# TensorE in program order within attention, and the sums that spread a tile's inverses moved to just ahead of its last value products

## The chip, the cores and the metric

The kernel runs on one core of a Trainium2 chip. A core has five instruction queues that work side by side: TensorE (PE, matrix products; its weight loads are listed apart as PEld), VectorE (DVE), ScalarE (ACT), GpSimdE (POOL) and SyncE (SP, which here issues the DMA transfers). Each of them takes its instructions in the order in which they were written into its queue, and waits for semaphores that others raise. The metric is the device time of one execution in microseconds.

## The reference

Three stages follow one another, on 4 x 576 = 2304 tokens of width 512 (8 heads of 64):

```python
# attention: causal, window of 128, linear bias by distance and head
scores = scale * q @ k.T + slope[h] * -abs(rel);  masked unless 0 <= rel < 128
attn = exp(scores - max);  attn /= sum(attn) + 1e-9
x = attn @ v
# mixture: 8 experts, all of them for every token, weighted by P
P = exp(x @ w_gate - max), then 8 rounds of row and column normalisation
out = sum over e of P[:, e] * (relu(x @ w1[e]) @ w2[e])
# a last two-layer stage
h = out @ w_in;  y = max(0.01 * h, h) @ w_out
```

## The kernel before

**Tiles and steps.** Attention works on 18 tiles of 128 tokens. A tile is done in two steps, `quad` 0 and 1, of four heads each: 36 steps, numbered here 0 to 35. For a step the kernel does, in this order of the data:

- `scores` (L238): four products, two heads `n` by two halves `r` of the partitions, into two PSUM tiles `s[0]` and `s[1]`. The two heads of a PSUM tile use the same 64 rows of TensorE, the two PSUM tiles different ones. Then per head a VectorE operation (L243) that adds the bias and finds the minimum, and a ScalarE exponential (L247) that also sums a row. They write `e`.
- `probs_T` (L273, L275): eight transposes of `e` on TensorE into two PSUM tiles `pt`, and two ScalarE copies from these to `pb`.
- `values` (L288): eight products of `pb` and `v` into `o`. After a tile's second step a VectorE operation (L296) multiplies `o` by the inverse row sums and writes the tile `acc[i]`.
- `inverses`, once for each tile: ScalarE adds a small number to the row sums (L256), VectorE takes the reciprocal (L257), eight small products (L260) spread it over the partitions into `rt`, and ScalarE copies that to `rb` (L263).

**Other work in the same stretch.** A list `fill` holds what the next stage needs: the scaling of the first expert's weights (ScalarE L550, L553, L427; GpSimdE L428, L577), the inputs' parts and sums, and the expert's products for the first token groups (TensorE L702 and L819, 12 or 6 to a piece, and L327 for the gate). The loop over the steps takes it out in portions, before and after the transposes:

```python
        filling(left)
        if scales:
            scales.pop(0)()
        probs_T(i, quad)
        if quad == 1:
            inverses(i)
        filling(left - 1)
        if scales:
            scales.pop(0)()
        values(i, quad)
```

Ahead of these lines stands `scores` of the step after. What the program's order gives one step, from one `scores` to the next, is called a turn below: scores of step k+1, fill, transposes of step k, fill, values of step k.

**What sets the order on an engine.** Not the program's order alone. A scheduler, which has a timeline of its own, places the instructions of each engine's queue, and may put an instruction ahead of earlier ones as long as the data allow it. After attention (L927) the experts' stage goes on for the rest of the span with products of L702 and L819.

**Buffers that tie the steps.** There are two PSUM tiles for `s`, so the scores of a step need the VectorE operations of the step before to be done; two for `pt` and `rt` together; one for `o`.

Of the kernel before, what the change touches and what calls it, by code (L numbers as in the profile page):

```python
# [31 lines left out]
def attn_moe_kernel(  # L32
# [83 lines left out]
    anchors = {}  # L116

# [105 lines left out]
    def scores(i, quad):  # L223
# [28 lines left out]
    def inverses(i):  # L252

        c = st[i]
        sm = c["sm"]
        nc.scalar.activation(out=sm, in_=sm, func=AF.Copy, bias=EPS)  # L256
        nc.vector.reciprocal(out=sm, in_=sm)  # L257
        rt = ps_t.tile([P, NP, P], F32, tag="pt", name="rt")
        for h in range(H):
            nc.tensor.matmul(rt[64 * (h % 2):64 * (h % 2) + 64, h // 2, :], sm[:, h:h + 1].to_broadcast([P, D]), ident,  # L260
                             start=True, stop=True)
        rb = c["rb"] = ap1.tile([P, NP, P], F32, tag="rb", name="rb")
        nc.scalar.activation(out=rb, in_=rt, func=AF.Copy)  # L263

    def probs_T(i, quad):
# [3 lines left out]
        for r in range(2):  # L269
            pt = ps_t.tile([P, 2, 2, P], F32, tag="pt", name="pt")  # L270
            for n in range(2):
                for b in range(nb):
                    nc.tensor.transpose(pt[:, n, b, :], c["e"][r][:, n, b * P:(b + 1) * P], ident)  # L273
# [4 lines left out]
    def values(i, quad):  # L278
# [5 lines left out]
        for n in range(2):  # L284
            for b, j in enumerate(kb):
                for r in range(2):
                    h = 4 * quad + 2 * n + r
                    nc.tensor.matmul(  # L288
# [4 lines left out]
                    )  # L293
# [22 lines left out]
    def logits(p):  # L316
# [6 lines left out]
        for s, terms in enumerate((first, second)):  # L323
            for k in range(n):
                todo = [(o, w, k0, i) for o, w, k0 in terms for i in range(4)]
                for m, (o, w, k0, i) in enumerate(todo):
                    nc.tensor.matmul(lp[:, s, k, :], XP[p][:, o, i // 2, i % 2, k * P:(k + 1) * P], w[:, k0 + i // 2, :],  # L327
                                     start=(m == 0), stop=(m == len(todo) - 1))
# [338 lines left out]
    def a_steps(ci, p):  # L667
# [6 lines left out]
        def step(g, j, d):  # L674
# [22 lines left out]
            for f in range(nf):  # L697
                ft = g * nf + f
                i = 0
                for kk in range(2):  # L700
                    for wp, xp in ((0, 0), (0, 1), (1, 0)):
                        nc.tensor.matmul(d[b][:, f, :], t[:, wp, kk, ft * P:(ft + 1) * P], XP[p][:, o, kk, xp, :],  # L702
                                         start=(i == 0 and f == 0 and j in FIRST), stop=(i == 5), skip_group_check=True)
# [94 lines left out]
    def b_steps(ci, p):  # L798
# [5 lines left out]
        def step(tt, j, d):  # L804
# [11 lines left out]
            for ft in range(2):  # L816
                h, f = Ht[ci, p, ft]
                for hp, wp in ((0, 0), (0, 1), (1, 0)):
                    nc.tensor.matmul(ps, h[:, o, hp, f, tt * P:(tt + 1) * P], w[:, wp, ft, :],  # L819
                                     start=(i == 0 and j in FIRST), stop=(i == 5), skip_group_check=True)  # L820
# [73 lines left out]
    for s, (i, quad) in enumerate(steps):  # L894
# [186 lines left out]
```

## Time and profile before

| what | value |
|---|---|
| median of 3 runs | 1959.84 us (1954.84 to 1960.63) |
| the profiled execution | 1959.59 us, span 1957.8 us |
| TensorE, share of the span | 97% |
| ScalarE, VectorE, GpSimdE | 70%, 67%, 68% |
| granted TensorE clock, mean | 0.995 |
| last value products of attention end | about 232 us into the span |

The span runs from the first to the last instruction; 1.8 us lie around it. Busy shares are averages over stretches with different limits; attention is the first eighth of the span, and the rest is the experts' stage, in which TensorE is busy nearly all the time.

### The profile page before, as it was taken

To read this page: it belongs to the slowest core of one execution; us is meant where nothing else is said; L and a number is where in the kernel's file an instruction comes from. 1 tells how busy PE (TensorE), PEld (TensorE's weight loads), DVE (VectorE), ACT (ScalarE), POOL (GpSimd) and SP (SyncE) were. 2 spreads that over 40 slices of the span, in tenths; PEclk is the share of its full clock that TensorE was granted. 3 is DMA by queue.
4 is the path that set the end of the run, shared out by engine and by line. 5 is a ranking of instruction groups with operands and counts; after the bars stand their busy time and mean duration, and the time that the engine had idled before them with its cause. 6 is when DMAs were issued, how large, how long until landed. Compare 5 with 4: busy or idle time off the path is not lost.

```text
span 1957.8 us, 45103 instructions
## 1 busy us (share of the span) xinstructions
PE 1890.2 (97%) x17725; PEld 1626.5 (83%) x17725; DVE 1320.9 (67%) x3604; ACT 1366.5 (70%) x3123; POOL 1327.3 (68%) x1142
## 2 busy tenths in 40 slices
PE   8999988999999999999999999999999998999998
PEld 6777667888898888889888888889889877889897
DVE  6444466676776767677676767666666777677876
ACT  7977666776767666676767676676666778776764
POOL 3843275868787786878677686775767686666743
PEclk9999999999999999999999999999999999999999
DMA  8432001120211211120111112101000000001001
GB/s 269 125 87 71 12 12 55 39 62 32 82 47 47 66 39 55 39 82 28 66 65 40 55 39 66 44 2 45 23 23 23 23 23 23 24 22 44 2 28 71
DMA packets 57861, 97.80 MB, mean 50 GB/s; under 512 B 3632, under 2 KB 22064, under 8 KB 57648
## 3 DMA queue, kind: packets, MB, share of 16 engines
q1 hardware_dynamic: 57648, 94.92, 14.9%
q8 instruction: 138, 2.26, 0.5%
q14 instruction: 75, 0.61, 0.1%
HBM read 81.81 MB, written 13.11 MB: 48 GB/s over the span
## 4 chain that ended last, share of the span: by engine, by line
PE 78%; ACT 7%; DVE 5%; DMA 5%; POOL 3%; issue 2%; POOLq 0%; SPq 0%; ACTq 0%; DVEq 0%
PE t L819 35%; PE s L702 21%; PE sq L702 15%; DMA raw<-in_moe_w_dram 3%; PE s L238 2%; PE o L288 2%; PE pt L273 1%; ACT junk L550 1%; POOL h L775 1%; DVE s L731 1%; PE rt L260 1%; ACT raw L553 1%; ACT w L427 1%; ACT e L247 1%; ACT xp L427 1%
## 5 line engine op out<-in xcount | busy, mean ns | idle before, releaser
L819 PE MATMUL t<-w,h 128*128 128x256 f16 x7560 | 985.1, 273 | 22.9 <-ACT part L829 10.3
L702 PEld LDWEIGHTS <-w 128*128 128x128 f16 x8400 | 759.1, 98 | 120.3 <-issue 35.0
L819 PEld LDWEIGHTS <-h 128*128 128x128 f16 x7560 | 730.2, 98 | 125.6 <-issue 33.9
L702 PE MATMUL s<-xp,w 128*128 128x256 f16 (+1 forms) x4908 | 620.3, 263 | 20.3 <-ACT q L726 10.4
L832 DVE SCALAR_TENSOR_TENSOR acc<-t,pu,acc 128x256 f32<-128x256 f32 x864 | 407.9, 479 | 220.3 <-PE t L819 173.3
L775 POOL TENSOR_TENSOR h<-s,h 128x1024 f16<-128x1024 f32 x180 | 388.2, 2157 | 136.8 <-ACT h L772 95.7
L702 PE MATMUL sq<-xp,w 128*128 128x256 f16 (+1 forms) x3492 | 447.5, 262 | 6.2 <-ACT q L714 4.5
L830 POOL TENSOR_TENSOR acc<-acc,part 128x256 f32<-128x256 f32 x324 | 235.6, 729 | 292.9 <-ACT part L829 260.6
L428 POOL TENSOR_TENSOR w<-raw,w 128x512 f16<-128x512 f32 x240 | 277.7, 1168 | 42.3 <-ACT w L427 41.9
L731 DVE SCALAR_TENSOR_TENSOR h<-sq,h 128x512 f16<-128x512 f32 (+1 forms) x348 | 190.6, 552 | 82.4 <-ACT h L756 47.6
L829 ACT ACTIVATE part<-t,pu 128x256 f32<-128x256 f32 x324 | 152.5, 471 | 109.0 <-PE t L819 100.1
L772 ACT ACTIVATE h<-s 128x1024 f16<-128x1024 f32 x180 | 189.6, 1053 | 42.2 <-DVE s L731 41.3
L718 DVE SCALAR_TENSOR_TENSOR sq<-sq,q 128x256 f32<-128x256 f32 x348 | 148.4, 427 | 72.0 <-PE sq L702 57.0
L714 ACT ACTIVATE q<-s 128x256 f32<-128x256 f32 x366 | 138.3, 379 | 73.0 <-PE s L702 60.4
L427 ACT ACTIVATE w<-raw 128x512 f16<-128x512 f32 x240 | 148.2, 628 | 8.3 <-PE t L819 6.0
L731 DVE SCALAR_TENSOR_TENSOR s<-sq,s 128x256 f32<-128x256 f32 x348 | 145.1, 417 | 2.1
L750 ACT ACTIVATE h<-sq 128x512 f16<-128x512 f32 x174 | 103.2, 593 | 55.4 <-PE t L819 28.9
L731 DVE SCALAR_TENSOR_TENSOR s<-sq,q 128x256 f32<-128x256 f32 x348 | 130.3, 416 | 12.4 <-ACT q L726 10.6
L550 ACT ACTIVATE junk<-raw 128x512 bf16<-128x512 f32 x160 | 100.2, 626 | 48.2 <-DMA raw<-in_moe_w_dram 47.1
L718 DVE SCALAR_TENSOR_TENSOR sq<-s,q 128x256 f32<-128x256 f32 x174 | 74.5, 428 | 86.6 <-ACT q L714 78.2
L756 ACT ACTIVATE h<-sq 128x256 f16<-128x256 f32 x174 | 65.9, 379 | 65.1 <-DVE sq L718 58.2
L553 ACT ACTIVATE raw<-raw,sr 128x512 f32<-128x512 f32 x160 | 102.4, 714 | 3.8 <-DVE sr L422 3.4
(137 smaller groups left out, 1785.8 us busy)
## 6 DMA issues: line engine op xcount, KB each, us to landing
raw<-in_moe_w_dram SPq DMA_DIRECT2D x32, 1024.0 KB, 5.1
k_t<-in_k_dram SPq DMA_DIRECT2D x16, 512.0 KB, 3.8
raw<-in_moe_w_in_dram SPq DMA_DIRECT2D x16, 512.0 KB, 3.6
raw<-in_moe_w_out_dram SPq DMA_DIRECT2D x16, 512.0 KB, 3.5
q_t<-in_q_dram SPq DMA_DIRECT2D x18, 256.0 KB, 3.7
v_t<-in_v_dram SPq DMA_DIRECT2D x18, 256.0 KB, 2.7
acc<-in_v_dram SPq DMA_DIRECT2D x18, 256.0 KB, 6.6
out_dram<-acc SPq DMA_DIRECT2D x18, 256.0 KB, 2.0
```

The source lines that it names most:

```text
L427: nc.scalar.activation(out=hi, in_=src, func=AF.Copy)
L428: nc.gpsimd.tensor_tensor(out=lo, in0=src, in1=hi, op=ALU.subtract)
L702: nc.tensor.matmul(d[b][:, f, :], t[:, wp, kk, ft * P:(ft + 1) * P], XP[p][:, o, kk, xp, :], start=(i == 0 and f == 0 and j in FIRST), sto ...
L714: nc.scalar.activation(out=q[:, k], in_=ps, func=AF.Copy, scale=CS)
L718: nc.vector.scalar_tensor_tensor(out=block(k), in0=ps, scalar=CS, in1=q[:, k], op0=ALU.mult, op1=ALU.add)
L731: nc.vector.scalar_tensor_tensor(out=out, in0=in0, scalar=sc, in1=in1, op0=op0, op1=op)
L772: nc.scalar.activation(out=h[:, 3:7, 0, :], in_=d["s"], func=AF.Copy)
L775: nc.gpsimd.tensor_tensor(out=h[:, 3:7, 1, :], in0=d["s"], in1=h[:, 3:7, 0, :], op=ALU.subtract)
L819: nc.tensor.matmul(ps, h[:, o, hp, f, tt * P:(tt + 1) * P], w[:, wp, ft, :], start=(i == 0 and j in FIRST), stop=(i == 5), skip_group_chec ...
L829: nc.scalar.activation(out=part, in_=ps, func=AF.Copy, scale=s)
L830: nc.gpsimd.tensor_tensor(out=dst, in0=dst, in1=part, op=ALU.add)
L832: nc.vector.scalar_tensor_tensor(out=dst, in0=ps, scalar=s, in1=dst, op0=ALU.mult, op1=ALU.add)
```

## The change

Every product of attention, and of the fill within it, is chained to the one written before it, by a dependency that costs no semaphore (both stand on TensorE's queue): on TensorE these instructions keep the program's order. Two small groups are not chained and may stand anywhere: the tiny products of the scaling factors (L402 and L421). The chain ends with attention. Besides, `inverses` is cut in two: its ScalarE and VectorE part now stands ahead of the transposes, its eight products and the copy of them (`spread_inverses`) behind the second portion of fill, right ahead of the value products.

```diff
+    in_order = [None]
+
+    def kept(ins):
+
+        if in_order:
+            if in_order[0] is not None:
+                tc.add_manual_dep(ins.ins, in_order[0],
+                                  mybir.DependencyInfo(mybir.DependencyClass.NoSync, mybir.DependencyReason.DATA),
+                                  reason="in order")
+            in_order[0] = ins.ins.name
...
-                nc.tensor.matmul(s[r][:, n, 0:W], qs[64 * r:64 * r + 64, h // 2, :],
-                                 c["k"][64 * r:64 * r + 64, h // 2, 0:W], start=True, stop=True)
+                kept(nc.tensor.matmul(s[r][:, n, 0:W], qs[64 * r:64 * r + 64, h // 2, :],
+                                 c["k"][64 * r:64 * r + 64, h // 2, 0:W], start=True, stop=True))
...
         nc.vector.reciprocal(out=sm, in_=sm)
+
+    def spread_inverses(i):
+
+        c = st[i]
+        sm = c["sm"]
         rt = ps_t.tile([P, NP, P], F32, tag="pt", name="rt")
...
-        probs_T(i, quad)
         if quad == 1:
             inverses(i)
+        probs_T(i, quad)
         filling(left - 1)
+        if quad == 1:
+            spread_inverses(i)
         if scales:
             scales.pop(0)()
         values(i, quad)
     assert not fill
+    in_order.clear()
```

The products of L260, L273, L288, L327, L702 and L819 are wrapped in `kept` in the same way. The number of instructions is the same on every engine. Because the scheduler works on all queues together, the orders on VectorE, ScalarE, GpSimdE and SyncE change too, all within attention; from about the end of attention on, every queue is the same as before.

TensorE around step 7 (the scores `s_657` and `s_658` are step 7's; `pt_682` and `pt_689` belong to step 6, `s_720` and `s_721` to step 8). Before:

```order
L238 MATMUL s_657<-k_t_421,qs_423 128x256 x2
L273 MATMUL pt_682<-ident_81,e_586 128x128 x2
L238 MATMUL s_658<-k_t_421,qs_423 128x256 x2
L273 MATMUL pt_682<-ident_81,e_586 128x128 x2
L421 LDWEIGHTS onesb_94
L421 MATMUL st_405<-b_388,onesb_94 128x2
L273 MATMUL pt_689<-ident_81,e_587 128x128 x4
L238 MATMUL s_720<-k_t_578,qs_580 128x256 x2
L238 MATMUL s_721<-k_t_578,qs_580 128x256 x2
L402 LDWEIGHTS e_535
L402 MATMUL mt_559<-identb_86,e_535 1x128
L288 MATMUL o_703<-pb_687,v_t_356 64x128
```

And with the change:

```order
L249 MATMUL s_657<-k_t_421,qs_423 128x256
L249 MATMUL s_658<-k_t_421,qs_423 128x256
L249 MATMUL s_657<-k_t_421,qs_423 128x256
L249 MATMUL s_658<-k_t_421,qs_423 128x256
L289 MATMUL pt_682<-ident_81,e_586 128x128 x4
L289 MATMUL pt_689<-ident_81,e_587 128x128 x4
L304 MATMUL o_703<-pb_687,v_t_356 64x128
L304 MATMUL o_703<-pb_694,v_t_356 64x128
```

The four scores stand together, in turn from one PSUM tile and the other, where before they were two pairs with other work between; and the scores of step 8, which stood ahead of step 6's value products, now stand behind all eight of them.

ScalarE around step 6 (`e_586`, `e_587`: exponentials of step 6; `w0`, `w1`: casts of the weights; `raw`: their scaling; `pb`: the copies that the value products need). Before:

```order
L247 ACTIVATE e_586,sm_583<-e_586,mn_582 128x256 x2
L247 ACTIVATE e_587,sm_583<-e_587,mn_582 128x256 x2
L263 ACTIVATE rb_638<-rt_629 128x512
L427 ACTIVATE xp0_118<-acc2_102 128x2x128
L247 ACTIVATE e_659,sm_583<-e_659,mn_656 128x256 x2
L275 ACTIVATE pb_687<-pt_682 128x512
L247 ACTIVATE e_660,sm_583<-e_660,mn_656 128x256
L275 ACTIVATE pb_694<-pt_689 128x512
L247 ACTIVATE e_660,sm_583<-e_660,mn_656 128x256
L553 ACTIVATE raw_234<-raw_234,sr_230 128x512 x4
L247 ACTIVATE e_722,sm_719<-e_722,mn_718 128x256 x2
```

And with the change:

```order
L443 ACTIVATE w0_526<-raw_234 128x512
L258 ACTIVATE e_587,sm_583<-e_587,mn_582 128x256 x2
L291 ACTIVATE pb_620<-pt_615 128x512
L291 ACTIVATE pb_627<-pt_622 128x512
L279 ACTIVATE rb_643<-rt_634 128x512
L443 ACTIVATE w1_737<-t2_699 128x512
L443 ACTIVATE w1_740<-raw_236 128x512
L443 ACTIVATE xp0_118<-acc2_102 128x2x128
L443 ACTIVATE w1_743<-raw_236 128x512
L443 ACTIVATE w1_746<-raw_236 128x512
L443 ACTIVATE w1_749<-raw_236 128x512
L258 ACTIVATE e_659,sm_583<-e_659,mn_656 128x256 x2
```

All fourteen casts of the first weight chunk now stand ahead of step 7's exponentials (`e_659`); before, the first cast stood behind step 8's. `t2_699` and `raw_236` are written by GpSimdE.

VectorE around step 4 (`e` from `s` is one head's bias and minimum, `mn` its read-out; `vmx` reads the values of one tile, `acc_107` those of tile 7, `acc_117` of tile 17). Before, step 4's last three heads are the three `e` rows here (its first stands just ahead of them):

```order
L243 ISA e,mn<-s,dist 128x256
L243 ISA mn 128x1
L221 TENSOR_REDUCE vmx<-acc_107 128x1
L243 ISA e,mn<-s,dist 128x256
L243 ISA mn 128x1
L404 TENSOR_REDUCE k<-mt 1x1
L243 ISA e,mn<-s,dist 128x256
L243 ISA mn 128x1
L221 TENSOR_REDUCE vmx<-acc_108 128x1
```

With the change, this stands ahead of step 4's first head (the last row):

```order
L232 TENSOR_REDUCE vmx<-acc_112 128x1
L232 TENSOR_REDUCE vmx<-acc_113 128x1
L410 TENSOR_REDUCE m<-vmx 128x1
L327 TENSOR_SCALAR wg<-wg,srg 128x32
L232 TENSOR_REDUCE vmx<-acc_114 128x1
L268 RECIPROCAL sm<-sm 128x8
L232 TENSOR_REDUCE vmx<-acc_115 128x1
L328 CAST wgs<-wg 128x4x8
L232 TENSOR_REDUCE vmx<-acc_116 128x1
L232 TENSOR_REDUCE vmx<-acc_117 128x1
L329 TENSOR_TENSOR wgs<-wg,wgs 128x4x8
L254 ISA e,mn<-s,dist 128x256
```

All eighteen reads of the values stand ahead of step 4; before, the last of them stood ahead of step 6.

## Rows read from the trace of the kernel before

**Rows 1.** Busy us (and count) of PE, PEld, DVE, ACT, POOL by stretch; PEclk, DMA.

```profile
20.00:80.00 60.00, 57.75 (x469) 41.52 (x470) 34.54 (x162) 56.84 (x171) 39.79 (x38) 1.00 0.57 178
80.00:190.00 110.00, 109.52 (x1002) 80.44 (x1000) 58.63 (x207) 81.53 (x241) 50.97 (x46) 1.00 0.30 87
190.00:232.00 42.00, 42.00 (x428) 31.30 (x427) 18.05 (x66) 26.82 (x76) 3.17 (x2) 1.00 0.09 26
...
300.00:1950.00 1650.00, 1610.06 (x15213) 1418.26 (x15212) 1161.49 (x3013) 1145.08 (x2497) 1179.79 (x992) 1.00 0.13 42
```

**Rows 2.** The same for line 238 (scores) on TensorE alone: PE busy, clock, DMA.

```profile
80.00:190.00 110.00, 27.86 (x132) 1.00 0.30 87
190.00:232.00 42.00, 6.97 (x34) 1.00 0.09 26
```

**Rows 3.** Timeline of TensorE: start, us, engine, line, operation, out<-in, shapes, count.

```profile
35.67 1.13 PE L238 MATMUL s<-k_t,qs 64*128 64x256 f32 x8
36.73 0.43 PE L288 MATMUL o<-pb,v_t 128*64 128x128 f32 x2
...
37.24 1.09 PE L260 MATMUL rt<-ident,sm 128*64 128x128 f32 x16
38.16 1.04 PE L288 MATMUL o<-pb,v_t 128*64 128x128 f32 x14
39.14 1.13 PE L238 MATMUL s<-k_t,qs 64*128 64x256 f32 x4
...
42.10 0.66 PE L273 MATMUL pt<-ident,e 128*128 128x128 f32 x4
...
144.17 1.47 PE L702 MATMUL s<-xp,w 128*128 128x256 f16 x12
```

**Rows 4.** Timeline behind the first of these scores: VectorE and ScalarE.

```profile
36.84 0.42 DVE L243 CUSTOM_DVE_ANT_0 e<-s,dist 128x256 f32<-128x256 f32 x1
...
37.30 0.51 ACT L247 ACTIVATE e<-e,mn 128x256 f32<-128x256 f32 x1
...
37.81 0.49 ACT L247 ACTIVATE e<-e,mn 128x256 f32<-128x256 f32 x1
```

**Rows 5.** Timeline at 66 us: ScalarE's copy and the value product that waits for it.

```profile
66.09 0.60 ACT L275 ACTIVATE pb<-pt 128x512 f32<-128x512 f32 x1
66.56 0.65 ACT L427 ACTIVATE w<-raw 128x512 f16<-128x512 f32 x1
...
66.74 0.98 PE L288 MATMUL o<-pb,v_t 128*64 128x128 f32 x13 [1.20 <-ACT pb L275]
```

**Rows 6.** Timeline of ScalarE: step 2's exponentials, the first weights; later a scaling of four.

```profile
14.76 0.51 ACT L247 ACTIVATE e<-e,mn 128x256 f32<-128x256 f32 x1 [0.57 <-DVE mn L243]
...
16.22 0.63 ACT L550 ACTIVATE junk<-raw 128x512 bf16<-128x512 f32 x1 [0.37 <-DMA raw<-in_moe_w_dram]
...
54.60 2.56 ACT L553 ACTIVATE raw<-raw,sr 128x512 f32<-128x512 f32 x4
```

**Rows 7.** Timeline of VectorE: one of the heads of step 4; the last of the 18 reads.

```profile
26.32 0.41 DVE L243 CUSTOM_DVE_ANT_0 e<-s,dist 128x256 f32<-128x256 f32 x1
...
35.13 0.66 DVE L221 TENSOR_REDUCE vmx<-acc 128x1 f32<-128x512 f32 x1
```

**Rows 8.** Groups on GpSimdE from 20 to 90 us: count, busy us, mean ns, idle before.

```profile
L428 POOL TENSOR_TENSOR w<-raw,w 128x512 f16<-128x512 f32 x12 | 13.8, 1171 | 0.0
...
L577 POOL TENSOR_TENSOR raw<-raw 128x512 f32<-128x512 f32 x4 | 5.1, 1285 | 0.0
```

**Rows 9.** Timeline of TensorE: the last value products of attention.

```profile
230.88 1.09 PE L288 MATMUL o<-pb,v_t 128*64 128x128 f32 x14
```

**Rows 10.** Timeline of TensorE at 10 us.

```profile
10.46 2.07 PE L238 MATMUL s<-k_t,qs 64*128 64x256 f32 x4
```

**Rows 11.** TensorE right behind attention, by stretch: busy us, granted clock, DMA.

```profile
236.00:238.00 2.00, 1.07 (x13) 0.65 0.00 0
238.00:240.00 2.00, 2.00 (x24) 0.50 0.03 8
```

More of the change, by code (lines that the diff above doesn't have):

```diff
@@ L257, in inverses @@
         nc.vector.reciprocal(out=sm, in_=sm)
+    def spread_inverses(i):
+        c = st[i]
+        sm = c["sm"]
         rt = ps_t.tile([P, NP, P], F32, tag="pt", name="rt")
         for h in range(H):
-            nc.tensor.matmul(rt[64 * (h % 2):64 * (h % 2) + 64, h // 2, :], sm[:, h:h + 1].to_broadcast([P, D]), ident,
-                             start=True, stop=True)
+            kept(nc.tensor.matmul(rt[64 * (h % 2):64 * (h % 2) + 64, h // 2, :], sm[:, h:h + 1].to_broadcast([P, D]), ident,
+                             start=True, stop=True))
         rb = c["rb"] = ap1.tile([P, NP, P], F32, tag="rb", name="rb")
@@ L272, in probs_T @@
                 for b in range(nb):
[L273 removed]
+                    kept(nc.tensor.transpose(pt[:, n, b, :], c["e"][r][:, n, b * P:(b + 1) * P], ident))
             pb = ap3.tile([P, 2, 2, P], F32, tag="pb", name="pb")
@@ L287, in values @@
                     h = 4 * quad + 2 * n + r
-                    nc.tensor.matmul(
+                    kept(nc.tensor.matmul(
                         o[64 * r:64 * r + 64, h // 2, :],
@@ L292, in values @@
                         start=(b == 0), stop=(b == len(kb) - 1),
-                    )
+                    ))
         if quad == 1:
@@ L326, in logits @@
                 for m, (o, w, k0, i) in enumerate(todo):
-                    nc.tensor.matmul(lp[:, s, k, :], XP[p][:, o, i // 2, i % 2, k * P:(k + 1) * P], w[:, k0 + i // 2, :],
-                                     start=(m == 0), stop=(m == len(todo) - 1))
+                    kept(nc.tensor.matmul(lp[:, s, k, :], XP[p][:, o, i // 2, i % 2, k * P:(k + 1) * P], w[:, k0 + i // 2, :],
+                                     start=(m == 0), stop=(m == len(todo) - 1)))
         back = small.tile([P, 1], F32, tag="lb", bufs=1, name="lb")
@@ L701, in step @@
                     for wp, xp in ((0, 0), (0, 1), (1, 0)):
-                        nc.tensor.matmul(d[b][:, f, :], t[:, wp, kk, ft * P:(ft + 1) * P], XP[p][:, o, kk, xp, :],
-                                         start=(i == 0 and f == 0 and j in FIRST), stop=(i == 5), skip_group_check=True)
+                        kept(nc.tensor.matmul(d[b][:, f, :], t[:, wp, kk, ft * P:(ft + 1) * P], XP[p][:, o, kk, xp, :],
+                                         start=(i == 0 and f == 0 and j in FIRST), stop=(i == 5), skip_group_check=True))
                         i += 1
@@ L818, in step @@
                 for hp, wp in ((0, 0), (0, 1), (1, 0)):
-                    nc.tensor.matmul(ps, h[:, o, hp, f, tt * P:(tt + 1) * P], w[:, wp, ft, :],
-                                     start=(i == 0 and j in FIRST), stop=(i == 5), skip_group_check=True)
+                    kept(nc.tensor.matmul(ps, h[:, o, hp, f, tt * P:(tt + 1) * P], w[:, wp, ft, :],
+                                     start=(i == 0 and j in FIRST), stop=(i == 5), skip_group_check=True))
                     i += 1
```

## The prediction

> **What bounds the kernel now.** I read the busy time by stretch first, then TensorE's timeline, then what the other engines do between two TensorE groups of one step. The reader is to see that the change can act in attention alone, the first 232 us of 1957.8: TensorE is 98% busy from 300 us on (1610 of 1650 us, [rows 1]) on queues that the change leaves alone, so what attention gains or loses moves the rest as a block. The last value products end at 230.88 + 1.09 = 232.0 us [rows 9]; that is the number which the change moves. Within attention TensorE shows no idle time from 80 to 232 us, and ScalarE is nearly full (56.84 of 60 us) from 20 to 80 us [rows 1]. Taken alone this says that TensorE is the bound.
>
> The timeline says what fills it. Four scores that run side by side take 1.06 us (a group of eight records, each product being two, from 35.67 to the next start at 36.73); two from one PSUM tile, on the same rows of the array, take as long for half the work (four records, 1.13 us at 39.14) [rows 3]. Line 238 takes 27.86 + 6.97 = 34.8 us for 166 records after 80 us [rows 2], where 166/8 groups of 1.06 would be 22.0. Value products with a first one torn off cost 0.43 us more for it [rows 3]. So TensorE is busy partly because its order is poor, and that order let it run ahead while other engines answered.
>
> **What the change removes.** Pairs become fours: 34.8 - 22.0 = 12.8 us of TensorE after 80 us; about as much before it, where ScalarE is the limit. Torn value products: one start of some 0.35 us in about 25 of 36 steps, 9 us. Some 22 us of TensorE's time in the stretch where it shows no idle time. The inverse sums cost the same 1.09 us [rows 3] in the new place; there they run while the copies are awaited, so I price their move at nothing; without that cover they would cost 18 x 1.05 = 19 us, which they cost before too.
>
> **What it adds: a closed turn.** With program order, the value products of step k wait for the ScalarE copies of step k, and the scores of step k+2 stand behind all of them. ScalarE has the exponentials of step k+1 ahead of these copies (order rows in the section on the change). A turn is then a chain through three engines:
>
> - start of the scores to VectorE's first head 36.84 - 35.67 = 1.17, to the first exponential 37.30 - 36.84 = 0.46 [rows 3, 4];
> - four exponentials at 0.49 each (37.30 to 37.81 is one, with its read-out, [rows 4]): 1.96;
> - first copy 0.47 to the next start, second copy 0.60 to its end, 0.05 to the product (66.09 + 0.60 = 66.69, then 66.74) [rows 5]: 1.12;
> - eight value products, 1.05 (sixteen records: 1.09 for as many at 37.24, [rows 3]), then the next scores.
>
> 1.17 + 0.46 + 1.96 + 1.12 + 1.05 = 5.8 us. TensorE's own work in a turn is 1.06 + 1.1 (eight transposes, twice 0.6 at 42.10) + 1.05, with 1.05 for the inverses in every second turn, and 1.3 for each twelve products of fill (1.47 for twelve less the tail of the last) [rows 3]. That is 3.2 to 4.3 us without fill and 5.8 to 6.9 with 24. A turn costs the larger of the two, and 0.3 to 1.0 more where ScalarE's queue has fill between the exponentials and the second copy. From the changed order, for turns 9 to 34 (the 26 from the scores of step 9 to those of step 35): fourteen turns with 24 products or the like at 6.6; seven with twelve at 6.05; turns 9 and 17 at 5.9 and 5.3; two empty ones at 5.3; turn 34 at 5.9. Sum 92.4 + 42.4 + 11.2 + 10.6 + 5.9 = 162.5 us. From the scores of step 35 to the last value product is one chain of 5.8, then transposes, copies and products again: 9.2.
>
> **The first nine turns.** Here the other queues decide, by the order in which they now stand.
>
> - ScalarE has two `junk` sums, which need the weights that land at 16.2 us, ahead of step 2's exponentials [rows 6]: these start at 17.5 instead of 14.8.
> - VectorE has all reads of the values ahead of step 4. The last was at 35.13 between other work, and step 4's third head at 26.32 [rows 7]. Eight reads of about 0.6 us behind step 3's heads and ahead of step 4's put step 4's first head at some 33.5 us and its exponentials at 34.
> - ScalarE's own queue from there, at 0.49 an exponential, 0.47 a copy, 0.61 a scaling (2.56 for four, [rows 6]) and 0.52 a cast (under the 0.65 of [rows 5]): 7.5 us to step 5, 9.5 to step 6, that is 51.
> - Then the cast `w1_737` waits for GpSimdE. GpSimdE can begin its casts at 40.5, and has ahead of `t2_699` nine casts of 1.17, six sums of 1.29 [rows 8] and two others, 20 us: 60. Two more sums to 62.5, then three casts on ScalarE: step 7's exponentials stand behind all of it and start at 64.5. ScalarE idles some 6 us, and nothing covers it, since step 7 is queued behind.
> - Turn 7 at 5.8, turn 8 at 6.9: scores of step 9 at about 76.
>
> **The sum.** 76 + 162.5 + 9.2 = 247.7 against 232.0: 15.7 us later. One term more: in the first 20 us the same pair of scores takes 2.07 us [rows 10], which at the second level takes 1.13 [rows 3]: TensorE's lower clock. Behind attention it fell to 0.50 after stretches with TensorE busy 1.07 of 2 us [rows 11]. In turns 1 to 9 TensorE has 3 to 4 us of work in 6 to 9; I take half clock in the three of them that the chain decides, 1.06 + 0.5 or so each: 4.5 us. Below it is 0, above it is all nine turns, 14. Total about +20 us: 1957.8 + 20, with the 1.8 around the span 1980 us. The profiled run (1959.59) and the median (1959.84) agree to 0.25 us, so the forecast is the same against the median. The turn is known to some 0.4 us, which over 26 turns is 10, and the early walk to 8: the forecast alone holds 1964 to 2000. The DMA loads of q, k and v change places on SyncE's queue by a few positions; after 20 us the DMA is busy at 0.57 and less [rows 1], so I price that at nothing; a load that came late for one turn would cost its 2 to 3 us once.
>
> The Trainium skill, page "TensorE: Matmul & The Clock Gate", section "Why this matters for your kernels", says that idle gaps between bursts of products put the clock back to half, and advises against them. It speaks against this change; the rows at 10 us and behind attention agree. By it, with half clock in all turns, 14 us in the first nine and 26 x 1.5 in the others would come on top of the 15.7, and the sum would be about 2028.
>
> **Rivals.**
>
> *TensorE was the bound (faster).* For it: no idle time in 152 us, and 22 us of its work go away there. Then the end moves with TensorE's time, and what ScalarE holds early stays as it is: 1959.6 - 22 = 1938. It decides where the copies are done before TensorE comes to the value products, that is where the turn's chain is under the 5.8 to 6.9 of TensorE's work; a chain shorter by 0.6 in all filled turns would do for most of it. Against it: the wait at 66.74, 1.20 us for a copy [rows 5], in a stretch with free choice of order, and nine early turns with no fill at all.
>
> The Trainium skill, page "TensorEngine Tiling (Array Packing)", section "Key Properties", says that tiles on different rows of the array load and multiply in parallel; the 1.06 us for four against two agree. By it alone the sum would be this rival's.
>
> *Early loss and later gain cancel (no change).* Before, the 26 steps from 9 to 35 ran under a TensorE without slack; if turns come out at 5.9 on average, since ScalarE's fill falls into the gaps, 26 x 0.35 = 9 us come back and the clock term is nil: 1959 to 1966.
>
> *The clock stays low through most of attention (slower still).* Each chain then holds scores, values and transposes at double: 1.5 us more in 20 to 26 turns, on top of 15.7 and up to 14 in the early ones: 2010 to 2030. Against it: from turn 10 on TensorE has 75% to 100% of a turn to do.
>
> That the order doesn't do as it says is excluded by the order rows, but for the two small groups that aren't chained.
>
> **How the numbers follow.** Forecast 0.60; TensorE the bound 0.20; cancelled 0.12; low clock 0.08. A measurement of this kernel can tell about 0.3%, 6 us, from no change. Faster by more than that 0.21, within it 0.13, slower 0.66. The range 1948 to 2002 holds the forecast, the cancelled case and the nearer half of the two outer ones, and leaves out about 0.2.
>
> **What would show it.** Four scores together in 1.06 to 1.13 us, TensorE's busy time in attention down by 20 us or more while its end moves from 232 to about 250 us. TensorE's longest waits: value products for the ScalarE copies, in most turns; early, ScalarE waiting for GpSimdE at about 55 to 60 us. Step 4's exponentials from about 34 us, step 9's scores at about 76. Turns of 6 to 7 us in the middle. The prediction is wrong if the value products find their copies done, or if step 9 comes at 60 us or earlier. From 300 us on nothing but a shift.

## The result, and the profile after

Over four runs of each on the same chip the changed kernel takes 1983.37 us (1982.27 to 1984.06) against 1958.91 (1954.84 to 1960.63): a ratio of 1.0127, 95% interval 1.011 to 1.0145, so 1.3% slower. The forecast was 1980, in a range of 1948 to 2002.

The page of the changed kernel, its span, the busy time of the engines, and two of its lines in 40 slices of the span (a slice is 50 us; digits are tenths):

```profile
span 1982.3 us, 45132 instructions
...
PE 1870.0 (94%) x17725; PEld 1622.6 (82%) x17725; DVE 1314.3 (66%) x3604; ACT 1365.7 (69%) x3123; POOL 1327.2 (67%) x1142
...
PE   6788888999999999999999999999999999999998
...
PEclk8799989999999999999999999999999999999999
```

TensorE does the same 17725 products in 20.2 us less busy time (1890.2 before), and the span is 24.5 us longer (1957.8 before). The low digits stand in the first slices alone. The busy time by stretch, in the columns of [rows 1] and in answer to them:

```profile
20.00:80.00 60.00, 41.22 (x283) 30.60 (x279) 24.28 (x109) 40.59 (x114) 38.89 (x37) 0.74 0.47 154
80.00:190.00 110.00, 96.20 (x1030) 76.97 (x1030) 50.85 (x199) 79.16 (x235) 41.75 (x38) 1.00 0.25 73
190.00:232.00 42.00, 34.70 (x346) 26.75 (x343) 19.02 (x83) 28.79 (x90) 11.75 (x11) 1.00 0.30 89
...
300.00:1975.00 1675.00, 1630.02 (x15415) 1435.46 (x15413) 1174.30 (x3051) 1157.31 (x2523) 1199.57 (x1010) 1.00 0.13 41
```

From 20 to 80 us TensorE did 283 products instead of 469, and no engine is full: ScalarE, 56.84 of 60 us before, has 40.59. From 300 us on TensorE is 97% busy (98% before). The scores alone, in answer to [rows 2]: more of them fall into these two stretches now, and they take less.

```profile
80.00:190.00 110.00, 16.91 (x126) 10.68 (x128) 1.00 0.25 73
190.00:232.00 42.00, 8.34 (x60) 4.82 (x56) 1.00 0.30 89
```

25.25 us for 186 records are 1.09 us for eight: the fours. The timeline of TensorE in turns 7 to 10 (a turn is named by the step whose scores stand at its head), in answer to [rows 3]:

```profile
57.24 1.82 PE L249 MATMUL s<-k_t,qs 64*128 64x256 f32 x8
58.99 1.09 PE L289 MATMUL pt<-ident,e 128*128 128x128 f32 x8
64.86 2.45 PE L304 MATMUL o<-pb,v_t 128*64 128x128 f32 x16 [4.78 <-ACT pb L291]
67.24 1.94 PE L249 MATMUL s<-k_t,qs 64*128 64x256 f32 x8
...
89.01 1.09 PE L276 MATMUL rt<-ident,sm 128*64 128x128 f32 x16
89.94 1.04 PE L304 MATMUL o<-pb,v_t 128*64 128x128 f32 x16
90.91 1.14 PE L249 MATMUL s<-k_t,qs 64*128 64x256 f32 x8
```

At 60 us TensorE stands still for 4.78 us, ahead of value products that want a ScalarE copy, and the next scores come behind them; at 67 us they take 1.94 instead of 1.1, at the lower of the two clocks (1.2 instead of 2.4 GHz; granted 0.50 from 64 to 68 us). The reason that the copy is late is this piece of ScalarE's timeline: a weight cast `w` waits for GpSimdE, step 7's exponentials (L258) stand behind all five weight casts, and step 6's copies `pb`, which the value products want, stand behind these exponentials.

```profile
59.27 0.63 ACT L443 ACTIVATE w<-t 128x512 f16<-128x512 f32 x1 [3.03 <-POOL t L593]
59.81 0.62 ACT L443 ACTIVATE w<-raw 128x512 f16<-128x512 f32 x1
60.33 0.40 ACT L443 ACTIVATE xp<-acc 128x256 f16<-128x256 f32 x1
60.64 1.73 ACT L443 ACTIVATE w<-raw 128x512 f16<-128x512 f32 x3
62.27 0.49 ACT L258 ACTIVATE e<-e,mn 128x256 f32<-128x256 f32 x1
...
64.23 1.06 ACT L291 ACTIVATE pb<-pt 128x512 f32<-128x512 f32 x2
```

Who waits for whom in attention, 0 to 260 us (us in total, times, longest):

```profile
...
ACT e L258 <- DVE mn L254: 40.3, 24, 4.9
DVE e L254 <- PE s L249: 31.0, 26, 4.7
...
PE o L304 <- ACT pb L291: 18.4, 19, 4.8
PE rt L276 <- ACT pb L291: 15.5, 11, 4.8
```

These are three sides of one ring: TensorE waits 33.9 us for ScalarE's copies, VectorE 31.0 for scores, ScalarE 40.3 for VectorE's minima.

Where the time goes is seen best from the start of the first value product of a step. The table has it for all kernels of this study (each from its profiled execution; the medians and ratios are against runs of the kernel before on the same chip, 1956.8 to 1958.9 us).

| kernel | step 8 | step 11 | from step 11 to 35 | last values end | median | ratio to before (95%) |
|---|---|---|---|---|---|---|
| before | 58.7 | 75.9 | 154.3 | 232.0 | 1958.9 | 1 |
| changed | 82.5 | 103.7 | 154.2 | 259.0 | 1983.4 | 1.0127 (1.0110 to 1.0145) |
| fours alone | 65.9 | 84.8 | 147.7 | 233.5 | 1954.9 | 0.9993 (0.9980 to 1.0005) |
| chain, inverses in the old place | 82.6 | 106.5 | 163.8 | 271.4 | 1994.2 | 1.0184 (1.0169 to 1.0200) |
| changed, scores two steps ahead | 64.0 | 104.4 | 144.4 | 249.8 | 1972.8 | 1.0078 (1.0063 to 1.0093) |
| changed, reads held back | 75.5 | 104.7 | 153.5 | 259.2 | 1980.7 | 1.0119 (1.0103 to 1.0134) |
| changed, second weights tied | 76.2 | 108.3 | 155.1 | 264.4 | 1985.8 | 1.0147 (1.0131 to 1.0163) |
| scores ahead, weights tied | 61.5 | 99.3 | 141.9 | 242.2 | 1964.2 | 1.0040 (1.0025 to 1.0055) |
| before, weights tied | 58.8 | 79.9 | 149.1 | 230.8 | 1944.7 | 0.9942 (0.9924 to 0.9959) |
| chained from step 10 | 58.0 | 93.1 | 154.1 | 248.3 | 1972.1 | 1.0080 (1.0061 to 1.0100) |
| chained up to step 9 | 81.2 | 104.9 | 145.8 | 253.7 | 1974.7 | 1.0091 (1.0068 to 1.0114) |
| changed, products added | 88.7 | 109.4 | 155.0 | 265.5 | 1986.6 | 1.0150 (1.0132 to 1.0168) |
| chained from 10, fill free | 59.2 | 78.5 | 153.7 | 233.3 | 1954.7 | 0.9985 (0.9976 to 0.9995) |
| before, tied, late fours | 58.7 | 77.6 | 146.6 | 225.2 | 1945.2 | 0.9944 (0.9927 to 0.9960) |

The loss is 23.8 us at step 8 and 27.8 at step 11. In between it grows to 34.4 at step 23, and at step 35 it is 27.7 again: over the middle as a whole, though not turn by turn, a chained turn is as long as a step was before. The end of attention moves by 27.0, the whole kernel by 24.5, so some 2 us come back behind attention; in the other chained kernels of the table the whole time moves by 2 to 5 us less than the end of attention.

### The profile page after: what moved, and what is told of

Its sections match the earlier page's. It is cut to its first block, busy times and chain, and to the rows that moved or that the text cites. A ratio compares the mean times of both kernels' runs of the same rounds, so it can differ in the third digit from the quotient of the medians.

```text
span 1982.3 us, 45132 instructions
## 1 busy us (share of the span) xinstructions
PE 1870.0 (94%) x17725; PEld 1622.6 (82%) x17725; DVE 1314.3 (66%) x3604; ACT 1365.7 (69%) x3123; POOL 1327.2 (67%) x1142
## 4 chain that ended last, share of the span: by engine, by line
PE 71%; ACT 9%; DMA 6%; POOL 5%; DVE 5%; issue 3%; SPq 0%; POOLq 0%; DVEq 0%; ACTq 0%
PE t L835 34%; PE s L718 19%; PE sq L718 14%; DMA raw<-in_moe_w_dram 4%; ACT e L258 2%; ACT junk L566 2%; POOL w L444 1%; PE o L304 1%; POOL h L791 1%; DVE s L747 1%; PE s L249 1%; ACT raw L569 1%; DMA acc<-in_v_dram 1%; PE rt L276 1%; POOL xp L444 1%
## 5 line engine op out<-in xcount | busy, mean ns | idle before, releaser
L747 DVE SCALAR_TENSOR_TENSOR s<-sq,q 128x256 f32<-128x256 f32 x348 | 129.9, 414 | 12.1 <-ACT q L742 10.6
L734 DVE SCALAR_TENSOR_TENSOR sq<-s,q 128x256 f32<-128x256 f32 x174 | 74.4, 428 | 85.7 <-ACT q L730 77.3
```

The costliest lines, as they stand in the source:

```text
L734: nc.vector.scalar_tensor_tensor(out=block(k), in0=ps, scalar=CS, in1=q[:, k], op0=ALU.mult, op1=ALU.add)
L747: nc.vector.scalar_tensor_tensor(out=out, in0=in0, scalar=sc, in1=in1, op0=op0, op1=op)
```

## The experiments

The theories: (1) the **closed turn** of the prediction, value products that wait for their own step's copies with the next scores behind them; (2) **early queues**, the orders on VectorE, ScalarE and GpSimdE in the first nine turns; (3) the move of the inverses; (4) the lower clock. One more came up on the way: (5) the **fill in the chain**, expert products whose inputs come late from GpSimdE and which all of attention now stands behind.

Moving the inverses without the chain leaves every engine's order of instructions as it was before, so that kernel wasn't run: the move can act only together with the chain.

**Fours alone.** Before, with the four scores of a call chained to each other and to nothing else:

```diff
     def scores(i, quad):
+        in_order[0] = None
         for n in range(2):
-            for r in range(2):
-                nc.tensor.matmul(s[r][:, n, 0:W], ...
+            for r in (1, 0):
+                kept(nc.tensor.matmul(s[r][:, n, 0:W], ...
```

> The kernel before, with one thing of the change: the four scores of one call are chained to each other and nothing else is, so the products of other kinds may stand between the calls as before. It tells what fours are worth without the closed turn. Rival 'TensorE was the bound': scores' busy time after 80 us falls from 34.8 us to between 22 and 30 (not all calls come out as fours, since the scheduler decides what stands between), and the whole time falls by that, 5 to 12 us against the kernel before. Closed turn (the loss of the change comes from value products that wait with the scores behind them): no loss here, time within 6 us of the kernel before or below it, attention ends at 220 to 234 us. If this run is 20 us slower, the order of the scores alone does the harm and both are wrong.

No difference that can be told. The steps from 11 to 35 are 6.6 us shorter, but 8.9 us were lost up to step 11. The scores took 32.77 us for 175 records after 80 us, against 34.8 for 166: few calls came out as full fours. TensorE's products become cheaper and the time stays. Why the first steps lose time isn't shown.

**The inverses in their old place.** The changed kernel, with

```diff
-        if quad == 1:
-            inverses(i)
         probs_T(i, quad)
-        filling(left - 1)
         if quad == 1:
+            inverses(i)
             spread_inverses(i)
+        filling(left - 1)
```

> The changed kernel with the inverses back in their old place (both halves between the transposes and the second portion of fill), all products still chained. It tells the chain from the move of the inverses. Closed turn and early queues alike: the chain does it, and the time stays within 8 us of the changed kernel's 1983. The moved inverses as the cause: back to about 1960. The prediction's price for the move was nothing, which asks for a difference under 6 us.

11 us slower still: outside what either theory expected, and outside the prediction's price of nothing for the move. The waits on TensorE in all of attention in this kernel:

```profile
PE rt L276 <- ACT pb L291: 23.6, 16, 6.4
PE o L304 <- ACT pb L291: 20.5, 18, 4.0
```

44.1 us for the two together against 33.9 in the changed kernel. The inverses take a PSUM tile of the same two as the transposes, so they wait for a copy of these; in the chain the fill that could run meanwhile stands behind them. The move is worth 10 us under a chain, and cannot be the cause of the loss.

**Scores two steps ahead.** The changed kernel, with

```diff
     scores(*steps[0])
+    scores(*steps[1])
...
-            scores(*steps[s + 1])
...
+        if s + 2 < len(steps):
+            scores(*steps[s + 2])
         values(i, quad)
```

> The changed kernel, but the scores are written two steps ahead: those of steps 0 and 1 before the loop, those of step s+2 right ahead of the value products of step s, so that they no longer stand behind products that wait for ScalarE's copies. Chain and moved inverses stay. Closed turn: it is opened, the 172.8 us from the scores of step 9 to those of step 35 shrink towards TensorE's own work (about 146 to 155 us), attention ends at 222 to 238 us and the time is 1945 to 1962. Early queues alone (the loss is made by the orders on VectorE, ScalarE and GpSimdE in the first nine turns, where those engines are waited for): the scores of step 9 still come after 70 us and the time is 1972 to 1985.

10.5 us back. The time lies just within what early queues alone had, but their sign fails: step 9's scores came at 56.4, not after 70. Values of step 8 come at 64.0 instead of 82.5, which is 18.5 of the 23.8 us lost up to there, and from step 11 on it is 9.8 us faster than the changed kernel. The 18.5 us aren't the closed turn's alone, though: the edit moves the other queues as well, and ScalarE has two weight casts ahead of step 7's exponentials here, where the changed kernel has fourteen. No run opens the turn and leaves these orders as they were. And all that was won early is gone at step 11. TensorE's timeline in this kernel, then GpSimdE's, then ScalarE's:

```profile
65.51 0.83 PE L718 MATMUL s<-xp,w 128*128 128x256 f16 x6
81.64 0.37 PE L718 MATMUL s<-xp,w 128*128 128x256 f16 x1 [15.30 <-ACT xp L443]
83.84 1.23 PE L718 MATMUL s<-xp,w 128*128 128x256 f16 x5 [1.83 <-POOL xp L444]
```

```profile
74.67 2.25 POOL L444 TENSOR_TENSOR w<-raw,w 128x512 f16<-128x512 f32 x2
76.89 0.71 POOL L490 TENSOR_TENSOR sx<-acc,sx 128x256 f32<-128x256 f32 x1
77.57 2.25 POOL L444 TENSOR_TENSOR w<-raw,w 128x512 f16<-128x512 f32 x2
79.79 0.71 POOL L490 TENSOR_TENSOR sx<-acc,sx 128x256 f32<-128x256 f32 x1
81.67 2.12 POOL L444 TENSOR_TENSOR xp<-sx,xp 128x1024 f16<-128x1024 f32 x1 [1.17 <-ACT xp L443]
```

```profile
80.54 1.06 ACT L443 ACTIVATE xp<-sx 128x1024 f16<-128x1024 f32 x1 [6.28 <-POOL sx L490]
```

The first expert products want `xp`, the split inputs of the first token groups; their sums `sx` stand on GpSimdE between weight casts `w`, and the last is done at 80.5. All attention that is ready to run waits behind these products. This is where theory 5 comes from.

**Reads held back.** The changed kernel, with VectorE's eighteen `vmx` reads tied behind the heads of the scores written last:

```diff
-        nc.vector.tensor_reduce(out=vmx[:, i:i + 1], in_=acc[i], ...
+        ins = nc.vector.tensor_reduce(out=vmx[:, i:i + 1], in_=acc[i], ...
+        if heads:
+            tc.add_manual_dep(ins.ins, heads[-1].ins.name, ...
```

> The changed kernel, with the eighteen VectorE reads of the values tied behind the heads of the scores written last, so that they can't all stand ahead of step 4's heads. Nothing else is altered. Early queues: step 4's exponentials start at about 28 to 31 us instead of 33.6, and the time falls by 2 to 6 us, to 1977 to 1981. Closed turn alone, or if ScalarE and GpSimdE bind the first nine turns in any case: step 9's scores stay at 77 us and the time within 2 us of 1983.

Step 4's exponentials start at 32.6 instead of 33.6, later than the 28 to 31 expected. Step 9's scores come at 70.2 instead of 77.3 (here nine casts, not fourteen, stand ahead of step 7's exponentials), with the turn still closed; then the chain waits for the inputs again (ScalarE 5.26 us for GpSimdE's `sx` at 76 to 81 us), the values of step 11 come 1.0 us later than in the changed kernel, and attention ends within 0.2 of it. The whole time is 2.7 us lower, within what two such comparisons can differ by. So the early queues set part of the pace of the first nine turns, but mending them in this way only brings the wait for the inputs forward.

**Second weights tied behind the inputs.** The changed kernel, with the casts and sums of the first expert's second weight matrix (`W[1][0].whole()`, eleven jobs on GpSimdE) written behind the first token groups' inputs and held there on ScalarE and GpSimdE:

```diff
-    fill = ... + W[1][0].scale() + W[1][0].whole()
+    fill = ... + W[1][0].scale()
...
                     fill += xin[p].parts(1) + a_steps(0, p) + [lambda p=p: logits(p)]
+                if p == 0:
+                    fill += W[1][0].whole() + [W[1][1].load]
...
+        if late:
+            behind(c, 0)
+            behind(s, 1)
```

> The changed kernel, with the seven casts and four sums of the first expert's second weight matrix tied behind the split inputs of the first token groups on ScalarE and GpSimdE (they stood ahead of part of them). TensorE's chain is left as it is, but for the later place of no product at all. Theory 'inputs behind weights': the first expert products in the chain wait for inputs whose sums and casts stand on GpSimdE behind weight casts that nothing needs yet, and all of attention waits behind these products. In this kernel the waits of the closed early turns still hide most of that, so by it step 9's scores come at 70 to 75 us instead of 77.3, attention ends at 252 to 257 us instead of 259.0 and the time is 1975 to 1981. Closed turn alone: the first turns are as long as they were, time within 2 us of 1983.

A miss for theory 5 as I had put it. Step 9's scores did come at 71.9, but the casts now run beside the first expert block, where they hold up VectorE (below, on the hardware); the chained products wait 3.98 us for ScalarE at 92.7 to 96.7, and step 12's scores come at 102.5 instead of 97.8. **The same with the scores ahead:**

> Both edits: scores written two steps ahead, and the second weight matrix's casts and sums tied behind the first split inputs. With the scores ahead alone, step 10's scores came at 62.0 us and step 11's at 89.6, and between them TensorE waited 15.3 us for a ScalarE cast of the inputs. Theory 'inputs behind weights': that stall shrinks from some 20 us above a usual turn to 8 or less, step 11's scores come at 68 to 78 us, attention ends at 227 to 238 us, and the time is 1950 to 1962, so no slower than the kernel before. Rival: the inputs can't come sooner, since attention's own values, or TensorE's chain before them, set their time; then step 11's scores stay at 86 to 90 us and the time at 1970 to 1975.

8.7 us better than the scores ahead alone, a little short of what was expected: the wait for ScalarE's cast of the inputs shrank from 15.30 to 5.26 us, and step 11's scores came at 79.2 instead of 89.6. **And the control, the kernel before with the same tie:**

> A control: the kernel before, with the same tie of the second weight matrix's casts behind the first inputs and no chain on TensorE. There the scheduler has the inputs ahead of nearly all weight casts already, and TensorE can take other products while it waits. By 'inputs behind weights' the edit is worth nothing here, 1952 to 1962. A gain of over 6 us would say that the tie is a gain by itself and that its worth in the other two kernels says nothing on the chain.

It gains 12 us by itself, which I had not expected. By what I had written, the worth of the tie in the other two says nothing on the chain then. What does is the shrunk wait in the trace, and the place of the gain: with the scores ahead the tie ends attention 7.6 us earlier (242.2 for 249.8). Here the gain isn't in attention's end (1.2 us earlier); some 6 us of it are there by 640 us, as the 4000th expert product comes at 641.9 instead of 648.0, and the rest between 640 and 1080 us (8000th: 1070.5, was 1084.1). TensorE's mean granted clock over the span is 0.998, against 0.995, but that isn't the main part: one run of the kernel before had 0.998 too and took 1955.7 us. Why a tie in attention speeds up the later stage stays open.

**Chain in one part alone.** The changed kernel with the chain begun at step 10 (`in_order` empty until then), and with the chain ended there:

```diff
+        if s == 10:
+            in_order.append(None)       # the other kernel: in_order.clear()
```

> The changed kernel, chained from step 10 on only; the steps 0 to 9 are as free as before, and TensorE's order up to about the scores of step 10 is that of the kernel before. Moved inverses stay. Theory 'early steps': the loss of the change is made before step 11, where ScalarE, VectorE and GpSimdE are behind and the chain turns each of their late results into a stall of all that follows; from step 11 on a chained turn lasts as long as a step did before (154.2 against 154.3 us from the values of step 11 to those of step 35). Then this kernel ends attention at 228 to 237 us and takes 1952 to 1963. Closed turn as the cause throughout (values that wait in every turn, with the next scores behind them): the 25 chained turns lose most of the 27 us by themselves, and the time is 1970 to 1982.

> The other half: the changed kernel, chained up to step 9 and free from step 10 on. Theory 'early steps': the loss is there already, values of step 8 at 78 to 86 us as in the changed kernel (82.5), attention ends at 250 to 260 us and the time is 1974 to 1985. Closed turn throughout: most of the loss is gone, 1957 to 1968. Both together would put it in between.

Chained up to step 9: the loss at step 8 is there, as "early steps" had it, and the free part behind makes up 8.5 us. Chained from step 10: steps 0 to 9 as before, step 11 to 35 as before (154.1), and yet 17.2 us lost by step 11, all of it behind step 8. That is a miss for "early steps"; the time falls into the range of "closed turn throughout", but not for its reason, as the rows below show. Either half alone makes more than half of the loss, so the two don't add up: a wait that comes first hides a later one. TensorE and GpSimdE in the kernel chained from step 10:

```profile
67.93 0.38 PE L718 MATMUL s<-xp,w 128*128 128x256 f16 x2
75.18 2.29 PE L718 MATMUL s<-xp,w 128*128 128x256 f16 x10 [6.88 <-POOL xp L444]
...
90.16 0.82 PE L718 MATMUL s<-xp,w 128*128 128x256 f16 x6 [2.64 <-ACT q L730]
```

```profile
69.65 3.41 POOL L444 TENSOR_TENSOR w<-raw,w 128x512 f16<-128x512 f32 x3
72.98 2.15 POOL L444 TENSOR_TENSOR xp<-sx,xp 128x1024 f16<-128x1024 f32 x1
```

Again the first expert products wait for `xp` behind casts. **The same, with the fill out of the chain** decides it:

```diff
-                    kept(nc.tensor.matmul(lp[:, s, k, :], ...
+                    nc.tensor.matmul(lp[:, s, k, :], ...
-                        kept(nc.tensor.matmul(d[b][:, f, :], ...
+                        nc.tensor.matmul(d[b][:, f, :], ...
-                    kept(nc.tensor.matmul(ps, h[:, o, hp, f, ...
+                    nc.tensor.matmul(ps, h[:, o, hp, f, ...
```

> The kernel chained from step 10 on only, with one thing less: the products of the fill (the gate's, and the experts' first and second) are no longer in the chain, so that only scores, transposes, values and inverses keep the program's order. In the kernel chained from step 10 the early steps were as before (step 10's scores at 48.2 us), and yet the values of step 11 came at 93.1 instead of 75.9: TensorE waited 6.9 us at 68 to 75 us for the first token groups' inputs, whose cast stands on GpSimdE behind weight casts, and 2.6 us at 88 for ScalarE. Theory 'fill in the chain': these stalls are the loss, since chained attention stands behind them; here the values of step 11 come at 76 to 84 us, attention ends at 228 to 240 us, and the time is 1950 to 1963. Closed turn (attention's own products in order are the loss): no change, 1968 to 1976.

As theory 5 expected: 17.5 us come back, and this kernel is 0.15% faster than the one before, which is no difference by the bound of 0.3%. TensorE in it:

```profile
71.60 1.54 PE L304 MATMUL o<-pb,v_t 128*64 128x128 f32 x16
73.07 1.13 PE L249 MATMUL s<-k_t,qs 64*128 64x256 f32 x8
74.13 1.09 PE L289 MATMUL pt<-ident,e 128*128 128x128 f32 x8
76.39 1.25 PE L718 MATMUL s<-xp,w 128*128 128x256 f16 x10 [1.16 <-POOL xp L444]
```

Values, scores and transposes pass the expert products that wait, and 1.16 us of the 6.88 are left. The inputs themselves come no earlier: the wait ends at 76.4 here, at 75.2 there. Attention's own products are in program order here, closed turns and all, from step 10 on: these alone cost nothing measurable. Not run is the changed kernel chained from the start with the fill left out, which would tell what the early turns cost by themselves.

**Products added, for the clock.** The changed kernel, with 24 products more in each of turns 1 to 8, whose result nobody reads:

```diff
+        if 1 <= s <= 8:
+            warm = ps_a.tile([P, 2, P], F32, tag="s2", name="warm")
+            for n in range(24):
+                kept(nc.tensor.matmul(warm[:, n % 2, :], ident, ident, start=True, stop=True))
         if quad == 1:
             spread_inverses(i)
```

> The changed kernel with 24 products more in each of the turns 1 to 8, between the transposes and the values (192 in all, into a PSUM tile that nobody reads, so the result is the same), where TensorE waits for ScalarE's copies. They should keep the granted clock at full in the stretch from 28 to 80 us, of which 30.6 us are at half clock in the changed kernel. They cost 2.6 us a turn at full clock, of TensorE's idle time. The prediction's clock term (half clock in the turns that the chain decides, 4.5 us): step 9's scores at 70 to 74 us instead of 77.3, time 1974 to 1980. If the clock costs nothing there, since the other engines set the pace: step 9's scores within 2 us of 77.3 and the time 1981 to 1986; later if the added products stand in the way.

The granted clock stays at full from 20 to 250 us, and the time is 3.2 us longer:

```profile
20.00:80.00 60.00, 60.00 (x582) 54.42 (x582) 24.13 (x111) 40.98 (x112) 33.41 (x32) 1.00 0.41 133
```

In the changed kernel this row has 0.74, that is (1 - 0.74) x 2 x 60 = 31 us of the 60 at half clock. Step 6's scores come 7.5 us later (52.6 for 45.1), since the added products stand in the way, and from there to step 9's it takes 28.0 us instead of 32.2. So the lower clock may cost some 4 us in these three turns; but the added products can stand in the way there too, and the orders on the other engines differ. It isn't the cause of the loss: with none of it from 20 to 250 us the loss is 29 us (1986.6 - 1957.5). What the clock alone is worth stays open.

**A candidate for the fastest.** Before, with the tie, and the four scores of a call chained to each other from the seventh tile on:

> A candidate for the fastest: the kernel before with the second weight matrix's casts tied behind the first inputs (1944.7), and the four scores of a call chained to each other, and to nothing else, from the seventh tile on. With fours alone, in all steps, the kernel lost 9 us up to the values of step 11 and won 6.6 from there to step 35 (147.7 instead of 154.3 us). If the early loss came from the early fours alone, this kernel is 3 to 7 us faster than the tie by itself: 1937 to 1942. If the gain was only that loss made up again, it is the same, 1942 to 1948.

The same time as the tie alone. Attention ends 5.6 us earlier (225.2), and by the 8000th expert product 1.0 us of that is left (1069.5 against 1070.5). The tie alone, at 0.9942 of before, beats both kernels.

## Why the prediction was right

**Direction, size and bound.** The forecast of about 20 us more was off by 3.4 in 1983.4. That TensorE was the bound, the faster rival, is out: 20.2 us of its busy time went away (22 predicted) and attention ended 27.0 us later. The two others are out too: the middle as a whole gave nothing back, and from 80 to 232 us the granted clock is 1.00.

**The first nine turns** came out nearly as walked through. Step 2's exponentials: 17.2 (predicted 17.5). Step 4's: 33.6 (34). Step 6's: 50.5 (51). Step 7's: 62.3 (64.5); ScalarE's wait for GpSimdE was 3.0 us, not 6. Scores of step 9: 77.3 (76).

**The middle was mis-sized, in the turns with fill.** The 26 turns from 9 to 34 took 172.8 us, not 162.5. The two empty turns took 5.25 us each (5.3 predicted), the seven with twelve products 43.2 in all (42.4). The fourteen with 24 products or the like took 100.0 instead of 92.4, 7.1 each instead of 6.6. What TensorE waited for from 95 to 250 us:

```profile
PE o L304 <- ACT pb L291: 6.3, 10, 1.1
PE rt L276 <- ACT pb L291: 5.8, 7, 1.5
PE t L835 <- ACT acc L842: 3.7, 4, 1.2
PE s L718 <- ACT q L742: 2.5, 3, 1.6
PE s L718 <- POOL xp L444: 1.9, 1, 1.9
...
```

The first two rows, 12.1 us for copies, are the prediction's chain; all but 1.5 us of them stand behind 189 us, in turns with little fill or none. The rows below, 10.1 us with two smaller ones, are the fill itself: expert products that wait until another engine has read the PSUM tile which they write next (8.2 us) or until their inputs `xp` are there (1.9), with attention queued behind them. The prediction took the larger of the chain and TensorE's work for a turn, and gave the fill no wait of its own. Before, with a free order, all waits of TensorE from 75 to 232 us come to 0.5 us.

**The end.** The last step was 8.9 us to the end (259.0 - 250.1; 9.2 predicted). So 259.0 stands against a predicted 247.7 + 4.5: 6.8 us too early. That the whole time is off by only 3.4 is luck in part: 2.5 us came back behind attention, and the median of the changed kernel is 0.7 us below its profiled execution (1983.4 against 1984.1). That attention's end moves the rest as a block held here to these 2.5 us; in the kernels before with the tie it didn't hold (12 us gained with an end 1.2 us earlier).

**The clock term** of 4.5 us can't be told apart. The half clock fell into the early turns as said, on 31 of 60 us, where three turns' worth were assumed; and the walk without it gave 76 for the scores of step 9, where 77.3 was measured with it. But two errors meet there. Step 7's exponentials came 2.2 us earlier than walked, and from them to step 9's scores it took 15.1 us instead of 11.5. The 3.6 us more are about what the term gives two turns, 3.1; but in turn 8 the inverse products, which wait for a copy, and a cast of the inputs stand in the chain too, which the walk didn't have there. The Trainium skill, page "TensorE: Matmul & The Clock Gate", section "Why this matters for your kernels", says that gaps between bursts put the clock to half: the trace agrees, 0.74 where TensorE was 41.22 of 60 us busy. The 14 us of the upper bound for the first nine turns are not to be seen.

**The inverses** were priced at nothing; within the chain the move is worth 10.8 us (1994.2 - 1983.4). That step failed. Nor do they run while the copies are awaited, as the prediction had it: they take one of the transposes' two PSUM tiles and so wait for a copy themselves (15.5 us in all), and of the turns 28 to 32, which have the same fill, those with inverses take 6.41 us and the others 5.74.

**What the prediction left out** is what the fill itself waits for. It counted the expert products in the chain by their own time alone. At the first of them, whose inputs come late, the changed kernel doesn't show it, as the early turns bring TensorE there only when the inputs are ready (80 to 86 us); it shows in the 10.1 us of the middle, and all at once as soon as the early turns are opened or freed: 15.30 us with the scores ahead, 6.88 chained from step 10. So "closed turn", together with the early queues, is right for the changed kernel's first eight steps, and how much of the 23.8 us belongs to either stays open (18.5 came back with the scores ahead and other orders, 7.0 with the reads held back). It is wrong as the whole story: behind it stood a second limit at nearly the same time, and over the middle as a whole the closed turn costs nothing against before, since TensorE's products are cheaper there.

## What to carry to other kernels

A fixed order on one engine turns each late operand of any product into a wait of all products behind it. So ask of every group in the order when its inputs are ready by the other engines' queues, above all of the filler that is there to cover waits; filler whose inputs can be late is to be left out of the chain (17.5 us in the kernel chained from step 10). Where undoing one part of a change brings back less than its share, look for a second limit at the same time, and undo both.

## What the runs showed of the hardware

VectorE operations with both inputs in SBUF can be held up by GpSimdE for far longer than they take. In the kernel chained from step 10, first VectorE, then GpSimdE:

```profile
81.35 4.96 DVE L747 SCALAR_TENSOR_TENSOR h<-q,h 128x768 f16<-128x768 f32 x1 [0.92 <-ACT h L754]
86.23 0.75 DVE L747 SCALAR_TENSOR_TENSOR s<-q 128x256 f32<-128x256 f32 x2
...
93.60 0.96 DVE L747 SCALAR_TENSOR_TENSOR h<-q,h 128x768 f16<-128x768 f32 x1 [0.91 <-ACT h L754]
```

```profile
80.95 4.54 POOL L444 TENSOR_TENSOR w<-raw,w 128x512 f16<-128x512 f32 x4
```

The same operation takes 4.96 us beside the four casts, and 0.96 with GpSimdE idle; it ends 0.8 us behind the last cast (86.31 against 85.49). ScalarE's `h`, which needs the operations behind it, waited 4.9 us, and TensorE 2.64 at 90 us for ScalarE. The kernel before has such a case too (5.20 us at 85 us, where its TensorE doesn't wait). It doesn't always go so: in the kernel with the scores ahead and the weights tied the two take turns. VectorE, then GpSimdE:

```profile
81.02 2.67 DVE L763 SCALAR_TENSOR_TENSOR s<-q,s 128x256 f32<-128x256 f32 x2
```

```profile
79.48 5.23 POOL L452 TENSOR_TENSOR w<-raw,w 128x512 f16<-128x512 f32 x4
```

Here an operation of 128x256 takes 1.3 us where it takes 0.42 alone, and a cast 1.3 instead of 1.1. The Trainium skill, page "SBUF — State Buffer", section "Who interferes with whom", says that a VectorE instruction with two SBUF inputs contends with a GpSimdE instruction that reads SBUF, and that one of them then waits. The rows agree; in the first case VectorE waited for a run of four casts, in the second for about one at a time. What decides between the two isn't shown.
